# State products of late chunks in bank c, root products inside the second layer, a split first gate product

## The chip, the core and the metric

The kernel runs on one core of one Trainium2 chip. The metric is the device time of one execution in microseconds. A core has several engines with a queue of instructions each: TensorE (PE, matrix products; PEld are its weight loads), VectorE (DVE), ScalarE (ACT), GpSimd (POOL) and SyncE (SP, which here issues the loads and stores). Each engine takes its instructions in order and waits on semaphores for the others.

## What is computed

The program is an attention block with a decaying state, followed by a feed-forward block. All values are float32.

```python
# B, H, S, D = 4, 8, 768, 48
for t in range(S):
    kt, vt, rt = k[:, :, t], v[:, :, t], r[:, :, t]
    cur = einsum('bhd,bhe->bhde', u[None] * kt, vt)
    y[:, :, t] = einsum('bhd,bhde->bhe', rt, state + cur)
    state = w[None, :, :, None] * state + einsum('bhd,bhe->bhde', kt, vt)
x = y.transpose(0, 2, 1, 3).reshape(B * S, H * D)          # 3072 tokens of 384
xn = x / sqrt(mean(x * x, axis=-1) + 1e-6) * rms_g
g, val = xn @ w_gate, xn @ w_val                           # 384 -> 1536
out = (g * sigmoid(g) * val) @ w_out                       # 1536 -> 384
```

## The kernel before

**Chunks.** The 768 steps are cut into NS = 12 chunks of L = 64 steps; a chunk holds the four batches, so 256 tokens. For each chunk s, `mixing(s)` (line 814) does the attention. TensorE makes, under the names that the plan gives its operations: the scores A of decayed k against decayed r, the outputs Y (scores times V, plus r times the state ST), the mean of squares r for the norm, and the state products U (k, scaled per token as KH, against V), which update ST. Chunks 0 and 1 have in addition a product E for the bonus term u, and they get their roots through GpSimd, VectorE and a `spread` product; chunk 0 also makes a table of powers for the tokens with a product called wk. From chunk 2 on (`brief`) the squares are summed by VectorE, one product r with a matrix of ones follows, and ScalarE takes the roots. The normed chunk is kept in two halves of rows, `xa` and `xb`, where `xb` is `xa` with its halves of 64 partitions exchanged by ScalarE.

**Feed-forward.** For chunks 0 and 1, `gate_val` (line 1019) makes gate and value of 128 features at a time: six matmuls with `wa` and `xa` and six with `wb` and `xb` into one bank (`product`, line 665), each on half of the rows; the operations are called g. For the very first weights (chunk 0, quarter 0) the products use the outputs before the norm, `yT` and its exchanged copy `yb`, and the root is multiplied in afterwards. `project` (line 1049, operations P) applies w_out. From chunk 2 on, two chunks are done together by a seven-product scheme: `group(s, m)` (line 1120) has the products f1 to f7 for one block of features of chunks s and s + 1, and `second_layer(s)` (line 1157) the products P1 to P7.

**PSUM.** There are four tiles of two banks: `bank_a`, `bank_b`, `bank_c` for the products and `at` for the attention. E of chunk 1 uses a product bank; A, Y, U and r use `at`, which a key "at" guards as one.

**Order.** Each operation is put into a `Plan` (line 181) with an engine, a cost, what it reads and writes and a function that issues it. The list `ORDER` (line 83), written out by hand from a search, says in which order they are issued, so each engine's queue has that order. Where the plan sees TensorE idle in the start, `warm` (line 1104) puts products of a matrix of ones there. `hint` and `final` go with the last TensorE operations.

**Loads.** `loads(s)` (line 757) loads one chunk: `CH` (k and r by channel), `TOK` (by token) and `V`. At most four of these large loads are in flight. There is one buffer of each, so `V` of the next chunk can be loaded when the state products U of this one, its last readers, are done. The weights come in pieces as 64-bit numbers (`piece`, raw_0 to raw_5), which VectorE, ScalarE and GpSimd turn into float32; the first ones are loaded between the inputs of chunk 0. Later `check` reads weights again to look at their low bits.

**Where state products stand.** In `mixing(s)` U follows the norm of its chunk: it waits for KH and V and for the tile `at`, into which it writes, and VectorE adds it to ST from there. Y of the next chunk needs ST. The main loop (line 1276) does for each pair the token sums, the six groups, `mixing(s + 2)`, `loads(s + 3)`, `second_layer(s)`, `mixing(s + 3)`, `loads(s + 4)`; ORDER then interleaves these.

Of the kernel before, what the change touches and what calls it, by code (L numbers as in the profile page):

```python
# [49 lines left out]
P = 128  # L50
# [12 lines left out]
L = 64  # L63
# [9 lines left out]
def feature_order():  # L73
# [10 lines left out]
    0, 4, 7, 5, 6, 8, 1, 11, 41, 10, 2, 16, 3, 42, 43, 21, 45, 26, 12, 46, 44, 76, 47, 49, 31, 48, 51, 52, 17, 13, 53,  # L84
    14, 50, 54, 58, 15, 98, 59, 55, 9, 101, 56, 18, 60, 36, 22, 23, 28, 62, 65, 19, 61, 29, 66, 20, 57, 67, 83, 63,
    24, 64, 27, 68, 111, 84, 121, 116, 25, 69, 70, 32, 124, 71, 72, 33, 122, 77, 30, 85, 88, 78, 34, 73, 193, 106, 86,
    123, 79, 74, 102, 35, 127, 80, 125, 81, 100, 93, 82, 103, 37, 38, 126, 39, 75, 104, 89, 107, 40, 129, 203, 131,
    198, 128, 105, 132, 94, 130, 112, 108, 133, 109, 90, 208, 110, 189, 134, 153, 118, 135, 113, 154, 114, 119, 136,
    155, 137, 99, 117, 115, 192, 138, 194, 120, 148, 139, 161, 95, 156, 140, 157, 141, 158, 142, 195, 196, 159, 143,
    197, 144, 162, 160, 146, 165, 87, 205, 163, 145, 200, 169, 147, 199, 164, 190, 149, 166, 206, 201, 167, 150, 168,  # L90
    202, 287, 277, 151, 173, 191, 216, 174, 272, 213, 170, 175, 152, 210, 177, 171, 176, 204, 172, 209, 211, 304, 178,
    282, 91, 214, 309, 226, 181, 207, 215, 225, 179, 182, 92, 212, 185, 183, 222, 184, 180, 186, 239, 223, 217, 270,
    249, 283, 96, 274, 219, 245, 275, 220, 218, 273, 224, 269, 246, 187, 276, 314, 278, 221, 250, 188, 288, 284, 279,
    247, 227, 350, 248, 289, 228, 253, 351, 240, 290, 257, 231, 251, 229, 258, 232, 252, 280, 254, 285, 353, 324, 255,
    233, 319, 234, 261, 329, 256, 281, 230, 262, 235, 286, 242, 259, 263, 260, 271, 265, 241, 352, 362, 266, 97, 243,
    291, 359, 292, 264, 356, 244, 376, 293, 267, 360, 268, 410, 296, 354, 363, 310, 297, 306, 305, 307, 357, 311, 334,
    355, 312, 298, 409, 300, 308, 358, 339, 299, 361, 301, 313, 389, 302, 294, 303, 315, 236, 390, 316, 295, 393, 391,
    563, 320, 321, 394, 326, 327, 364, 322, 567, 365, 344, 392, 317, 325, 368, 366, 369, 318, 377, 367, 370, 564, 401,
    371, 331, 323, 372, 328, 335, 565, 379, 378, 332, 238, 402, 373, 340, 341, 330, 342, 395, 589, 569, 566, 596, 374,
    345, 411, 380, 333, 576, 572, 381, 336, 237, 337, 575, 338, 568, 573, 595, 346, 570, 343, 574, 375, 622, 571, 383,  # L100
    623, 347, 396, 384, 385, 624, 348, 577, 349, 625, 578, 397, 579, 581, 398, 582, 407, 441, 399, 420, 580, 408, 442,
    403, 632, 400, 412, 590, 413, 635, 591, 414, 583, 584, 626, 443, 415, 449, 444, 592, 631, 594, 404, 585, 629, 634,
    593, 386, 405, 627, 450, 406, 633, 446, 628, 451, 445, 447, 452, 448, 648, 455, 417, 453, 597, 654, 460, 456, 387,
    457, 462, 461, 454, 459, 468, 463, 458, 465, 469, 586, 464, 466, 470, 471, 479, 472, 467, 481, 480, 630, 418, 388,
    474, 475, 636, 476, 473, 478, 482, 638, 487, 477, 484, 488, 639, 649, 483, 485, 419, 637, 423, 490, 486, 655, 489,
    416, 493, 491, 498, 494, 500, 499, 640, 495, 641, 421, 497, 506, 492, 501, 799, 507, 642, 422, 503, 496, 643, 426,
    502, 504, 509, 505, 508, 424, 512, 510, 425, 517, 513, 511, 429, 803, 514, 519, 518, 588, 516, 525, 520, 800, 522,
    526, 515, 650, 521, 523, 427, 428, 528, 524, 432, 527, 531, 529, 530, 536, 532, 802, 533, 538, 537, 535, 534, 651,
    539, 544, 801, 652, 541, 545, 430, 431, 540, 542, 433, 547, 543, 434, 546, 806, 438, 550, 548, 435, 808, 555, 601,
    551, 653, 552, 549, 556, 553, 644, 602, 603, 804, 554, 645, 831, 605, 598, 646, 811, 812, 557, 439, 558, 587, 604,  # L110
    599, 809, 436, 810, 437, 562, 440, 825, 606, 609, 561, 647, 832, 656, 600, 805, 612, 610, 559, 560, 611, 807, 858,
    613, 608, 657, 614, 813, 615, 617, 616, 658, 618, 814, 619, 815, 817, 818, 862, 826, 660, 661, 819, 607, 859, 685,
    659, 687, 686, 620, 621, 693, 688, 690, 694, 820, 695, 689, 691, 664, 696, 692, 860, 699, 697, 698, 704, 700, 861,
    706, 705, 662, 701, 828, 870, 703, 707, 827, 708, 702, 663, 709, 867, 667, 712, 710, 665, 711, 715, 713, 868, 714,
    718, 716, 666, 717, 670, 723, 719, 721, 725, 724, 720, 722, 731, 726, 727, 732, 733, 668, 728, 669, 871, 673, 742,
    729, 730, 734, 884, 891, 737, 735, 743, 744, 738, 739, 671, 741, 750, 745, 829, 746, 751, 736, 752, 672, 747, 740,
    864, 676, 833, 761, 748, 749, 753, 756, 754, 762, 763, 757, 755, 1035, 758, 674, 769, 760, 764, 765, 770, 1036,
    675, 766, 771, 759, 780, 767, 768, 772, 830, 775, 773, 781, 776, 863, 774, 777, 869, 890, 782, 865, 779, 677, 788,
    783, 866, 785, 789, 778, 678, 784, 786, 682, 816, 679, 791, 787, 794, 792, 790, 793, 795, 872, 797, 796, 798, 834,
    837, 1037, 821, 1042, 838, 840, 839, 835, 683, 873, 836, 680, 681, 684, 822, 845, 876, 874, 877, 1038, 875, 1039,  # L120
    878, 841, 879, 846, 880, 1044, 881, 849, 842, 844, 1048, 882, 893, 883, 823, 894, 848, 1045, 850, 885, 886, 824,
    851, 887, 1047, 847, 852, 843, 853, 923, 1061, 854, 921, 895, 1068, 888, 922, 855, 896, 889, 924, 897, 856, 1040,
    1094, 1067, 926, 892, 857, 929, 927, 925, 930, 1041, 931, 932, 928, 940, 933, 1046, 935, 941, 1043, 942, 936, 937,
    898, 939, 948, 943, 944, 949, 934, 950, 899, 938, 945, 903, 900, 959, 946, 947, 951, 954, 952, 1098, 953, 1049,
    960, 955, 957, 956, 1051, 961, 958, 963, 962, 1050, 382, 1062, 964, 901, 967, 965, 966, 970, 968, 1053, 902, 1054,
    973, 904, 906, 969, 971, 905, 978, 974, 1097, 980, 979, 975, 972, 977, 982, 981, 1095, 1055, 1096, 1056, 983, 976,
    986, 984, 985, 1064, 987, 1063, 1120, 1069, 989, 909, 1103, 988, 992, 990, 1107, 1065, 991, 997, 993, 1106, 1066,
    994, 999, 998, 995, 1104, 996, 1099, 1000, 907, 1126, 1005, 1101, 1100, 1002, 1006, 1001, 1003, 908, 912, 1008,
    1004, 1127, 1007, 1011, 1009, 1010, 1016, 1012, 910, 1014, 1013, 1018, 1017, 1015, 911, 1020, 1019, 915, 1052,
    1275, 1021, 1024, 1022, 1023, 1027, 913, 1105, 914, 1102, 1030, 1025, 918, 1028, 1029, 1031, 1108, 1026, 1032,  # L130
    1033, 1034, 1073, 1070, 916, 917, 1071, 1121, 1074, 1122, 1057, 1076, 1109, 1058, 1112, 1059, 1271, 1075, 1081,
    1110, 1272, 1113, 919, 1111, 1072, 920, 1114, 1082, 1077, 1115, 1274, 1116, 1060, 1117, 1085, 1078, 1083, 1119,
    1079, 1273, 1080, 1281, 1118, 1084, 1086, 1278, 1129, 1277, 1130, 1280, 1087, 1123, 1089, 1124, 1157, 1090, 1088,
    1159, 1158, 1160, 1091, 1132, 1125, 1133, 1131, 1092, 1276, 1297, 1093, 1162, 1304, 1165, 1163, 1279, 1161, 1166,
    1136, 1128, 1303, 1168, 1164, 1167, 1171, 1169, 1170, 1176, 1172, 1282, 1173, 1178, 1177, 1175, 1283, 1180, 1284,
    1179, 1134, 1330, 1135, 1181, 1174, 1139, 1184, 1182, 1137, 1183, 1187, 1185, 1138, 1190, 1188, 1142, 1186, 1334,
    1197, 1191, 1195, 1331, 1192, 1196, 1285, 1194, 1189, 1198, 1332, 1287, 1203, 1193, 1200, 1140, 1288, 1204, 1339,
    1199, 1201, 1141, 1206, 1202, 1298, 1145, 1209, 1207, 1337, 1205, 1286, 1216, 1210, 1333, 1208, 1214, 1289, 1218,
    1215, 1290, 1212, 1211, 1143, 1222, 1213, 1144, 1217, 1148, 1223, 1291, 1224, 1219, 1233, 1220, 1146, 1221, 1225,
    1228, 1226, 1234, 1235, 1229, 1147, 1230, 1151, 1241, 1227, 1232, 1236, 1237, 1242, 1299, 1243, 1231, 1238, 1292,  # L140
# [40 lines left out]
class Plan:  # L181
# [48 lines left out]
    def give(self, order, free, idle, hint, final):  # L230

        assert sorted(order) == list(range(len(self.ops)))
        start, busy = self.times(order, free), 0.0
        last = [i for i in order if self.ops[i][0] == "PE"][-4:]
        for i in order:
            if i == last[0]:
                hint()
# [1565 lines left out]
```

## Time and profile before

| | |
|---|---|
| time, median of 3 runs | 597.23 us (596.34 to 598.35) |
| the profiled execution | 596.35 us |
| its span, first to last instruction | 594.6 us |
| granted TensorE clock | 0.997 |
| TensorE busy | 583.1 us, 7226 matmul records |
| VectorE, ScalarE, GpSimd busy | 419.0, 295.1, 42.6 us |
| moved by DMA | 62.99 MB |

The span is the time from the first to the last instruction of one profiled execution; its own time is a little longer. A float32 matmul leaves two records, so twelve records are six matmuls. A row of a timeline has the start, the length, the engine, the source line, the operation, "out<-in" by the names of the tiles, the form and the number of instructions; at its end, where the engine had been idle, the length of that and what ended it stand in brackets. The line is that of a helper (L178) throughout, so rows are told apart by their tiles. In a product's form, 64*128 means 64 rows and 128 columns of weights, and 64x256 the moved operand.

### The profile page before, as it was taken

What the parts mean: (1) busy time and instruction counts of PE and PEld (TensorE: products, weight loads), DVE (VectorE), ACT (ScalarE), POOL (GpSimd) and SP (SyncE); (2) the same over time, 40 slices, a digit from 0 to 9 for tenths busy, and PEclk for the clock granted to TensorE, in tenths of its full rate; (3) what the DMA queues carried; (4) which work ended last, traced back from release to release, by engine and by line L of the source; (5) the groups of instructions that cost most, each with busy time, mean ns of one, the idle gap of its engine ahead of it and who ended that gap; (6) DMA issues with size and microseconds to landing.
All of it is one profiled execution on the core that took longest, in us unless ns stands there. A gap on an engine that the chain in (4) does not pass through costs nothing.

```text
span 594.6 us, 16484 instructions
## 1 busy us (share of the span) xinstructions
PE 583.1 (98%) x7226; PEld 512.5 (86%) x7226; DVE 419.0 (70%) x622; ACT 295.1 (50%) x713; POOL 42.6 (7%) x40
## 2 busy tenths in 40 slices
PE   8899999999999999999999999999999999999995
PEld 6688887667888899888999888899888899988995
DVE  7869798988767887666885576796665676355641
ACT  6855784847266443743383267564364652131300
POOL 2443143210000000000000000000000000000000
PEclk9999999999999999999999999999999999999998
DMA  8866664231422143131404404302621201210001
GB/s 281 321 237 237 255 219 151 96 101 46 148 90 79 59 155 81 54 107 63 133 7 128 167 29 142 134 7 53 228 77 54 64 9 26 80 41 15 2 23 37
DMA packets 22768, 62.99 MB, mean 106 GB/s; under 512 B 2944, under 2 KB 9760, under 8 KB 21280
## 3 DMA queue, kind: packets, MB, share of 16 engines
q1 hardware_dynamic: 21920, 61.36, 30.9%
q8 instruction: 58, 0.95, 0.6%
q10 hardware_dynamic: 768, 0.49, 0.3%
q14 instruction: 22, 0.18, 0.1%
HBM read 56.04 MB, written 4.72 MB: 102 GB/s over the span
## 4 chain that ended last, share of the span: by engine, by line
PE 94%; DMA 2%; ACT 1%; DVE 1%; issue 0%; POOL 0%; SPq 0%; ACTq 0%; DVEq 0%; POOLq 0%
PE bank_b L178 32%; PE bank_a L178 27%; PE bank_c L178 25%; PE at L178 10%; DMA raw<-in_wkb_dram 1%; DMA raw<-in_wka_dram 1%; DMA chan<-in_chan_dram 0%; ACT ST L178 0%; DVE ms L178 0%; DVE KH L178 0%; POOL wb L178 0%; ACT ku L178 0%; ACT yT L178 0%; ACT wk L178 0%; POOL ms L178 0%
## 5 line engine op out<-in xcount | busy, mean ns | idle before, releaser
L178 DVE TENSOR_TENSOR gv<-bank_b,m 128x512 f32<-128x512 f32 x90 | 62.2, 691 | 60.5 <-PE bank_b L178 58.6
L178 ACT ACTIVATE gv<-gv 128x256 f32<-128x256 f32 (+1 forms) x60 | 31.0, 524 | 70.5 <-DVE gv L178 70.3
L178 DVE TENSOR_TENSOR gv<-bank_c,gv 128x512 f32<-128x512 f32 x60 | 41.5, 691 | 23.8 <-PE bank_c L178 23.2
L178 PE MATMUL bank_b<-xa,wa 64*128 64x256 f32 x444 | 55.1, 381 | 0.0
L178 ACT COPY m<-bank_a 128x512 f32<-128x512 f32 (+1 forms) x35 | 20.0, 571 | 64.2 <-PE bank_a L178 38.0
L178 PEld LDWEIGHTS bank_b<-xa,wa 64*128 64x128 f32 x444 | 42.1, 187 | 6.1 <-DVE TOK L178 0.7
L178 PE MATMUL bank_a<-xa,wa 64*128 64x256 f32 x372 | 46.2, 380 | 0.0
L178 PE MATMUL bank_a<-xb,wb 64*128 64x256 f32 x372 | 45.6, 378 | 0.0
L178 PE MATMUL bank_a<-wo,h 128*128 128x192 f32 x264 | 45.6, 329 | 0.0
L178 PE MATMUL bank_b<-t,s 64*128 64x256 f32 x360 | 44.3, 378 | 0.0
L178 PE MATMUL bank_b<-t,wb 64*128 64x256 f32 x360 | 44.0, 377 | 0.0
L178 PE MATMUL bank_c<-t,s 64*128 64x256 f32 x360 | 44.0, 377 | 0.0
L178 PE MATMUL bank_c<-xb,s 64*128 64x256 f32 x360 | 43.9, 376 | 0.0
L178 PEld LDWEIGHTS bank_a<-wo,h 128*128 128x128 f32 x264 | 42.9, 190 | 0.8 <-issue 0.3
L178 ACT ACTIVATE MT<-dmask,du 128x64 f32<-128x64 f32 x160 | 41.5, 340 | 3.5 <-DVE du L178 3.4
L178 ACT ACTIVATE rows_out<-rows_out 128x384 f32<-128x384 f32 x72 | 39.8, 559 | 0.5
L178 PEld LDWEIGHTS bank_a<-xb,wb 64*128 64x128 f32 x372 | 35.8, 187 | 4.5 <-issue 0.3
L178 PEld LDWEIGHTS bank_a<-xa,wa 64*128 64x128 f32 x372 | 35.3, 187 | 4.7 <-issue 0.6
L178 ACT ACTIVATE gv<-bank_a 128x256 f32<-128x256 f32 x30 | 11.5, 385 | 54.5 <-PE bank_a L178 54.5
L178 DVE TENSOR_TENSOR h<-gv 128x256 f32<-128x256 f32 (+1 forms) x60 | 32.5, 551 | 8.3 <-ACT gv L178 8.1
L178 PEld LDWEIGHTS bank_c<-xb,s 64*128 64x128 f32 x360 | 34.9, 187 | 4.0
L178 PEld LDWEIGHTS bank_b<-t,s 64*128 64x128 f32 x360 | 34.5, 187 | 4.3 <-issue 0.3
(183 smaller groups left out, 1099.6 us busy)
## 6 DMA issues: line engine op xcount, KB each, us to landing
chan<-in_chan_dram SPq DMA_DIRECT2D x11, 1024.0 KB, 5.7
TOK<-in_tok_dram SPq DMA_DIRECT2D x10, 768.0 KB, 4.3
V<-in_vpad_dram SPq DMA_DIRECT2D x12, 512.0 KB, 4.8
raw<-in_wot_dram SPq DMA_DIRECT2D x8, 576.0 KB, 5.6
rows_out<-in_wka_dram SPq DMA_DIRECT2D x12, 384.0 KB, 3.0
rows_out<-in_wkb_dram SPq DMA_DIRECT2D x12, 384.0 KB, 3.1
rows_out<-in_wot_dram SPq DMA_DIRECT2D x12, 384.0 KB, 3.4
raw<-in_wka_dram SPq DMA_DIRECT2D x6, 576.0 KB, 5.5
```

The lines of the kernel that those rows point to most:

```text
L178: return lambda *args, **kwargs: self.tc.keep_in_program_order(give(*args, **kwargs))
```

## The change

There are five edits and a new `ORDER`.

1. **State products apart from `mixing`.** `mixing` is cut into `mixing` (attention, squares and, for odd late chunks, the root product), `roots_of` (the sums of squares, the root product and the roots), `mixed` (norm and exchange) and `state` (decay of the state, U, the additions). For chunks 3 and later, `state` takes the tile `bank_c` and its keys in place of `at`. It is added after group 0 of a pair for the odd chunk and after group 2 (`SLOT`) for the even chunk, whose `mixing` also moves there.
2. **Root product of even chunks.** For even chunks from 4 on, `roots_of` is called within `second_layer`, just before P5, and writes half of bank b.
3. **Loads.** `V` of a chunk from 4 on is loaded after the state products before it (`load_values`), no longer within `loads`.
4. **First gate product.** With `SPLIT = 1` the first product of chunk 0 is given as four operations: the `wa` side for batches 0 and 1, then for 2 and 3, then the `wb` side likewise, each of six matmuls with 128 columns. `yb` gets keys of its own per pair of batches.
5. **Fillers and hint.** The fillers before the first data are 128 columns wide and four times as many; `unused` has another letter order; the branch hint comes one TensorE operation later.

```diff
-        last = [i for i in order if self.ops[i][0] == "PE"][-4:]
+        last = [i for i in order if self.ops[i][0] == "PE"][-3:]
...
-    def product(ps_, w, x, start):
+    def product(ps_, w, x, start, cols=slice(0, NT)):
...
-                    ps_[:, z, 0:NT], w[rows, cc, :], x[rows, cc, :], start=start and cc == 0,
+                    ps_[:, z, cols], w[rows, cc, :], x[rows, cc, cols], start=start and cc == 0,
...
-        add("SP", 1.5, [], ["V"], lambda: load_v(s), land=LAND, name=f"load v {s}")
         if s == max(EARLY) + 1:
             add("SP", 0.5, [], ["utab"], load_u, land=LAND)
+        if s < 4:
+            load_values(s)
+
+    def load_values(s):
+        add("SP", 1.5, [], ["V"], lambda: load_v(s), land=LAND, name=f"load v {s}")
...
-        bank, key = next_at()
+        bank, key = next_at() if s < 4 or s % 2 else (None, None)
...
+            if s < 4 or s % 2:
+                roots_of(s, bank, key)
...
+        if not brief:
+            mixed(s)
+            state(s)
+        elif s < NS - 1:
+            add("DVE", 0.95, ["TOKk", "wk"], ["KH"], lambda: state_k(s), port=True, name=f"h {s}")
+
+    def roots_of(s, bank, key):
+        for n in (2, 1):
+            add(
+                "DVE", 0.15 + 0.27 * n, ["sq1"], ["sq0"],
+                lambda n=n: dve.tensor_add(sq[:, 0:n], sq[:, 0:n], sq[:, n : 2 * n]), port=True, name=f"q {s}",
+            )
+        add(
+            "PE", 0.45, ["sq0", "sq1"], [key],
+            lambda: pe.matmul(bank[:, 0:NT], ones, sq[:, 0], start=True, stop=True), name=f"r {s}",
+            rows="full",
+        )
+        def roots():
+            act.activation(rms, bank[:, 0:NT], AF.Sqrt, scale=1.0 / DM, bias=eps)
+            silu_table()
+
+        add("ACT", 3.3, [key], ["diag"], roots, land=-TABLE, name=f"sqrt {s}")
+        add("DVE", 1.75, [], ["diag"], lambda: dve.reciprocal(rms, rms), name=f"inv {s}")
+
+    def mixed(s):
+        x = place(s)
+        if s > 1:
+            add("DVE", 0.95, ["diag", "yT0", "yT1"], [f"xa{x}"], lambda: scaled(s, rms, yT), port=True, name=f"x {s}")
         for z in range(2):
             add("ACT", 0.83, [f"xa{x}"], [f"xb{x}.{z}"], lambda z=z: exchange(s, z), name=f"xb {s}")
+
+    def state(s, tile=at, keys=("at", "at")):
...
-        next_at(), next_at()
-        add("PE", 0.97, ["KH", "V"], both, lambda: states(at), name=f"U {s}", rows="4")
+        if keys[0] == "at":
+            next_at(), next_at()
+        add("PE", 0.97, ["KH", "V"], list(keys), lambda: states(tile), name=f"U {s}", rows="4")
...
+    SPLIT = 1
...
+        if first and o < SPLIT:
+            for q in range(2):
+                cols, own = slice(2 * L * q, 2 * L * (q + 1)), [f"{keys[0]} {q}"]
+                add(
+                    "PE", 0.66, weight_keys("wa", i, o) + [f"yT{q}"] + [f"{keys[0]} 0"] * q, own + keys * (1 - q),
+                    lambda q=q, cols=cols: product(ps_, wa[i][:, o], yT, q == 0, cols), name=f"g {s} {i} {o}", rows=True,
+                )
+            for q in range(2):
+                cols, own = slice(2 * L * q, 2 * L * (q + 1)), [f"{keys[0]} {q}"]
+                add(
+                    "PE", 0.66, weight_keys("wb", i, o) + [f"yb{q}"], own,
+                    lambda cols=cols: product(ps_, wb[i][:, o], yb, False, cols), name=f"g {s} {i} {o}", rows=True,
+                )
+            keys = keys + [f"{keys[0]} {q}" for q in range(2)]
...
-    unused = list("bbaaacbbbbbb")
+    unused = list("baaaacbbbbbb")
...
-            for _ in range(int((until + 0.4 - 3.75) / 0.86)):
-                pe.matmul(bank[:, 0], ones, free_dims(ones, (0, 4), (1, P)), start=True, stop=True)
+            for _ in range(4 * int((until + 0.4 - 3.75) / 0.86)):
+                pe.matmul(bank[:, 0, 0:P], ones, ones, start=True, stop=True)
...
         if not last:
+            roots_of(s + 2, bank_of["b"][:, 1], "b")
+            mixed(s + 2)
             mm("z", gs + out_keys("o1"), sum_1, w2(0), True, "P5")
...
+    SLOT = 2
...
             group(s, m)
+            if m == 0:
+                state(s + 1, bank_of["c"], bank_keys["c"])
+                if s + 2 < NS:
+                    load_values(s + 2)
+            if m == SLOT and s + 2 < NS:
+                mixing(s + 2), state(s + 2, bank_of["c"], bank_keys["c"]), load_values(s + 3)
...
-            mixing(s + 2), loads(s + 3)
+            loads(s + 3)
...
-            mixing(s + 3)
+            mixing(s + 3), mixed(s + 3)
```

In the order that results, U of chunks 3, 6, 7 and 9 stands directly before the scores A of the chunk after it, U of chunk 8 directly behind the outputs Y of its own chunk, and U of chunk 10 behind A of chunk 11. In the start the products U0, E1 and A1 follow each other (before: E1, U0, a gate product, A1), the second half of the first gate product stands behind `spread` and wk, and SP's queue has two weight pieces ahead of V of chunk 0 (before: one).

## The prediction

> **What bounds the kernel now.** I read the busy times by stage first, then TensorE's timeline in the middle, then the timelines of the start. In the stage view the columns are the stretch, its length, and the busy time (and instruction count) of TensorE, its weight loads, VectorE, ScalarE and GpSimd, then clock, DMA share and GB/s.
>
> ```profile
> 0.00:36.00 36.00, 31.31 (x676) 24.02 (x677) 29.75 (x68) 24.33 (x57) 13.63 (x22) 1.00 0.86 302
> 36.00:588.00 552.00, 551.78 (x6554) 488.44 (x6550) 388.87 (x554) 270.82 (x657) 28.99 (x19) 1.00 0.29 94
> 588.00:594.60 6.60, 0.04 (x1) 0.00 (x0) 0.36 (x1) 0.00 (x0) 0.00 (x0) 0.78 0.14 38
> ```
>
> From 36 us to 588 us TensorE is idle for 0.22 us. There is no wait to remove in 552 us: there the time is what TensorE's instructions take, and only their cost or their order can change it. The first 36 us have 4.7 us of idle TensorE, with the DMA engines at 0.86. The last 6.6 us are stores and the end of the program, which the diff leaves alone.
>
> Order has a price. TensorE works in three forms: products on two halves of 64 rows (shown as 64*128), attention work on blocks of 64 or 48 rows and columns (48*64, 64*64, 48*48), and whole-array work (128*128). The timeline (start, length, instruction) around chunk 5's root product:
>
> ```profile
> 173.45 1.46 PE L178 MATMUL bank_b<-t,s 64*128 64x256 f32 x12
> 174.75 1.46 PE L178 MATMUL bank_a<-third,wb 64*128 64x256 f32 x12
> 176.14 0.70 PE L178 MATMUL at<-sq,ones 128*128 128x256 f32 x2
> 176.77 1.57 PE L178 MATMUL bank_b<-xa,wa 64*128 64x256 f32 x12
> 178.17 1.46 PE L178 MATMUL bank_c<-t,s 64*128 64x256 f32 x12
> ```
>
> Lengths overlap, so steps from start to start count. A product between products takes 174.75 - 173.45 = 1.30. The one before the root product takes 1.39, the root product 0.63, the one after it 1.40. The same view in the second layer, where a root product stands among whole-array work, and where state products (at<-V,KH) stand alone:
>
> ```profile
> 303.92 0.59 PE L178 MATMUL at<-sq,ones 128*128 128x256 f32 x2
> 304.35 4.06 PE L178 MATMUL bank_a<-wo,h 128*128 128x192 f32 x24
> 308.25 4.06 PE L178 MATMUL bank_b<-wo,h 128*128 128x192 f32 x24
> 312.15 4.06 PE L178 MATMUL bank_a<-w,h 128*128 128x192 f32 x24
> 316.14 1.15 PE L178 MATMUL at<-V,KH 64*64 64x48 f32 x64
> 317.22 1.57 PE L178 MATMUL bank_b<-t,s 64*128 64x256 f32 x12
> 318.62 1.46 PE L178 MATMUL bank_a<-xa,wa 64*128 64x256 f32 x12
> ```
>
> There the root product takes 0.43. So a stay of it between products costs 0.63 - 0.43 + 0.09 + 0.10 = 0.40 for two changes of form, 0.20 each. The state products alone take 1.08 and lengthen their neighbours by 0.09 (3.99 for 3.90) and 0.10. Of their 1.08 about 0.14 is entering and leaving (the 64 records start 0.93 us apart, first to last, and the next instruction 0.15 later, where a group of the same form follows within 0.04). A stay in the attention form costs 0.34, or 0.17 per change.
>
> **The change, part by part. 1, order in the saturated stretch.** I count the changes of form in the order in which each program gives TensorE its work, from the first product of the second weight quarter on (35.0 us in the profile). Before: 82. After: 69. Between products and attention work they go from 39 to 38, between products and whole-array work from 22 to 21, between whole-array and attention work from 21 to 10. Six stays in the attention form vanish, because state products U are given beside scores A or outputs Y (U3 A4, U6 A7, U7 A8, Y8 U8, U9 A10, A11 U10), and even chunks' root products move beside second-layer work. Sum: 1 x 0.20 + 12 x 0.17 = 2.2 us less. The work itself is the same instructions, nothing covers this time, so all of it comes off the span if no wait takes its place.
>
> A rule of the Trainium skill bears on such merging. "Runtime: NRT & Kernel Launch", section "Instruction fetch mechanics", says that an engine's program comes in blocks of 16 KiB, 256 instructions, that the sequencer fetches ahead by DMA, and that this is mostly hidden. The page of this kernel shows the queue, 58 packets with 0.95 MB, 16 KB each, some 128 matmul records and their weight loads to a block:
>
> ```profile
> q8 instruction: 58, 0.95, 0.6%
> ```
>
> In the start it is not hidden. Two groups are cut in the middle, with nothing named as releaser:
>
> ```profile
> 13.31 0.67 PE L178 MATMUL bank_c<-MT,V 64*64 64x64 f32 x27 [0.57 <-issue]
> ...
> 29.13 0.81 PE L178 MATMUL at<-RR,chan 48*64 48x64 f32 x39 [0.71 <-issue]
> ```
>
> The two cuts are 254 matmul records apart, two blocks, so I take them for late blocks. Two blocks took 15.8 us; the second begins 127 records after 13.31, which counts to the middle of chunk 1's scores E, about 23.9, and took 5.3 us. A merged U and A is 128 records in 2.0 us, so a whole block can pass in little more than that. By the rule this costs nothing; by the row of the start it would cost up to 3 us each. In the saturated stretch the DMA share is 0.29 instead of 0.86, and outputs Y (128 records in 1.99 us) stand there ten times without a cut. I take 0 there, and keep the row for the start.
>
> **2, the start.** Here the change costs. (a) V of chunk 0 is loaded after two weight pieces instead of one, and first outputs wait for it already (0.44 us until 9.78, put down to that load). The queue:
>
> ```profile
> 3.90 0.33 SPq L178 DMA_DIRECT2D raw<-in_wka_dram  x1
> 4.85 0.33 SPq L178 DMA_DIRECT2D V<-in_vpad_dram  x1
> 5.55 0.33 SPq L178 DMA_DIRECT2D raw<-in_wkb_dram  x1
> ```
>
> A piece of 384 KB at the stage's 302 GB/s is 1.3 us, and issues there follow each other after 0.7 to 1.75, so V lands about 1 us later. Its outputs, then the scores and outputs of the second pair behind them in TensorE's queue, slip by as much. Of this the cut of 0.57 at 13.31 can absorb a part: +0.3 (0 to +1.0).
> (b) The first gate product is given by pairs of batches, and its second half (the xb side) now stands behind the spread and the table product wk. Before, this half ran at 17.01 to 18.50, while the mean square went through VectorE and GpSimd (spread at 20.05 after a wait of 0.83 for diag). Nothing else fills that hole, so 1.5 us move behind wk (21.21): +1.5. There they cover the wait of U0 for KH, 0.61 until 25.07: -0.6. By column count the halves cost the same (12 matmuls of 128 columns for 6 of 256). No row has 64*128 with 128 columns; the whole-array 128x128 filler takes 0.22 per matmul, half of the root product's 0.43, so I take +0.1, with +1.3 per side if the 12 weight loads hold it.
> (c) U0, E1 and A1 now follow each other: 192 records in 3 us, one and a half blocks, where one took 5.3 us. Before, a product of 1.66 stood between them and 0.71 + 0.17 was still lost at A1. I take 0.3 more than before (between -0.9, if the blocks fall well, and +2).
> Together +0.3 + 1.5 - 0.6 + 0.1 + 0.3 = +1.6. The twelve 128-column fillers at the very start replace three of 512 columns, the same columns, ahead of the first data: 0.
>
> **3, what is late next.** V and TOK of late chunks are now loaded after that chunk's state product, so their load starts when U ends. The tightest place is chunk 10: between the end of U9 and Y10 stand A10 and five products, 1.1 + 5 x 1.3 + 0.2 = 7.8 us. The page gives for the load:
>
> ```profile
> V<-in_vpad_dram SPq DMA_DIRECT2D x12, 512.0 KB, 4.8
> ```
>
> Behind the load on SP stand TOK, a weight check and chan; what they feed is needed later. With half a microsecond to issue, 5.3 of 7.8: hidden, 0, and about +1 if that load takes twice its median. The next tightest (U5 to Y6) has seven products between, 9.3 us. U in bank c needs c drained by VectorE first: at least one product stands between c's last writer and U, 1.3 us against one read of 0.69 (gv<-bank_c,gv). U's own three additions into ST (0.55 each, 1.7 together) then have at least two products, 2.7 us, before bank c is written again (tightest at U4). Both are hidden as long as VectorE, busy for 389 of 552 us, is not a microsecond behind; where it is, each place would cost a few tenths, and there are eight. The end differs only in where the branch hint is placed.
>
> **Sum.** -2.2 + 1.6 = -0.6. The profiled execution was 596.35 with a span of 594.6, so 1.75 lies outside it; after, span 594.0 and execution 595.8. The three runs have a median of 597.23 (596.34 to 598.35), 0.9 above the profiled one, and I forecast on their scale: 597.2 - 0.6 = 596.6.
>
> **Rivals.** *The start hides its losses* (0.26): blocks fall well, A1's 0.71 and 0.17 vanish and V's delay goes into the cut, so the start costs at most 0.3. For it: both cuts and U0's wait, 1.9 us together, are idle time that another order can fill. Against it: the hole of 17 to 20 us stays. Time: 597.2 - 2.2 + 0.2 = 595.2.
> *Instruction blocks in the start* (0.24), the one on the other side: U0, E1, A1 use up a block within 2.5 us of its beginning and TensorE waits till 5.3 us have passed, 2.8 lost where 0.9 was lost before, and the halves of the first product, which double their instructions, bring the next boundary forward into Y1 with another 1 to 2. Start +4.0, time 597.2 - 2.2 + 4.0 = 599.0; it decides once the start costs more than 2.2 + 1.8 = 4.0, and is slower at all from 2.2.
> *V10 late* adds 1 us to any case; alone it ends at 597.6 and is counted with no change.
> *No net effect*: the switches do not cost where I think, because TensorE would wait for VectorE or ScalarE instead. Against it: they are busy for 389 and 271 of 552 us. It lies within the likeliest case.
>
> **How the numbers follow.** A measurement of this kernel tells about 0.3% (1.8 us) from no change. The likeliest case, a start of +0.5 to +3.5, ends within it: 595.5 to 598.5, chance 0.50. Of the first rival some ends just inside, of the third case some just outside; I give faster 0.26, same 0.50, slower 0.24. Range: from 594.8 (start costs nothing, fewer switches at 0.20 each) to 598.8 (start +3.8).
>
> **What would show it.** Right: between 45 us and the last matmul no idle on TensorE, and that stretch about 2.2 us shorter for the same work; the first product of chunk 1 begins 1 to 2 us later than its 45.8 (after one U of 1.1 more in front of it); second halves of the first gate product behind wk; waits put down to issue in E1 or A1. Wrong: a wait of TensorE for V, KH or bank c in the saturated stretch, a start that ends no later than before, or cuts of the issue kind at merged U and A.

## The result and the profile after

The changed kernel takes 594.81 us (median of 20 runs, 593.09 to 597.04). The kernel before takes 597.75 us (20 runs, 595.33 to 600.69; the three shown ahead of the prediction are among them). The ratio is 0.9952, with a 95% interval of 0.9937 to 0.9966: 0.48% or 2.9 us faster, and the whole interval lies beyond the 0.3% that a measurement can tell from no change. I had forecast -0.6 us.

The profiled execution after took 594.46 us with a span of 592.7 us, against 596.35 and 594.6 before: 1.9 us less in each. The traces explain these 1.9 us. The other 1.0 us of the medians' difference is in neither: the profiled execution before was 1.40 us below the median of its 20 runs, the one after 0.35 us below.

The middle stage of the kernel after, in the columns of the prediction's stage view:

```profile
36.00:586.00 550.00, 549.39 (x6554) 491.29 (x6551) 384.99 (x554) 270.02 (x657) 28.94 (x19) 1.00 0.29 95
```

TensorE still sets the time: it is idle for 0.61 us of the middle 550 (0.22 of 552 before). Fixed times do not cut the two programs at the same work, so I cut both where the same TensorE operations are left: before at the first product of chunk 1 (45.80), after at U1, which stands in front of it now (46.33), and at the start of the last matmul group (583.98 and 582.75). Before:

```profile
0.00:45.80 45.80, 41.11 (x756) 32.22 (x758) 34.67 (x82) 29.31 (x70) 18.63 (x25) 1.00 0.78 272
45.80:583.98 538.18, 537.96 (x6449) 476.48 (x6446) 382.35 (x536) 265.84 (x644) 23.99 (x15) 1.00 0.28 93
583.98:594.60 10.62, 4.06 (x25) 3.77 (x24) 1.96 (x6) 0.00 (x0) 0.00 (x0) 0.86 0.18 48
```

After:

```profile
0.00:46.33 46.33, 42.12 (x811) 37.06 (x811) 37.04 (x82) 31.95 (x78) 18.81 (x25) 1.00 0.82 292
46.33:582.75 536.42, 535.81 (x6448) 479.67 (x6447) 376.79 (x537) 261.86 (x636) 23.09 (x15) 1.00 0.28 91
582.75:592.70 9.95, 4.07 (x26) 3.77 (x24) 1.43 (x4) 0.00 (x0) 0.00 (x0) 0.86 0.17 46
```

The second column gives the three differences: start +0.53, saturated stretch -1.76, end -0.67, together -1.90.

| part | forecast | in the traces |
|---|---|---|
| start | +1.6 | +0.53 |
| saturated stretch | -2.2 | -1.76 |
| end | 0 | -0.67 |
| sum | -0.6 | -1.90 |

**The saturated stretch.** TensorE's timeline of the kernel after, around U3, where scores now follow directly:

```profile
145.15 1.46 PE L179 MATMUL bank_b<-t,s 64*128 64x256 f32 x12
146.54 1.15 PE L179 MATMUL bank_c<-V,KH 64*64 64x48 f32 x64
147.51 1.13 PE L179 MATMUL at<-RR,chan 48*64 48x64 f32 x64
148.56 1.57 PE L179 MATMUL bank_a<-third,wb 64*128 64x256 f32 x12
```

The same view around U4, which stands alone in both kernels:

```profile
167.69 1.46 PE L179 MATMUL bank_b<-t,s 64*128 64x256 f32 x12
169.08 1.15 PE L179 MATMUL bank_c<-V,KH 64*64 64x48 f32 x64
170.16 1.57 PE L179 MATMUL bank_a<-third,wb 64*128 64x256 f32 x12
```

From start to start, U alone takes 170.16 - 169.08 = 1.08, and A alone 1.09 at every place of both traces where it has no neighbour of its form. Side by side they take 148.56 - 146.54 = 2.02. The product in front of a stay takes 1.39 and the one behind it 1.40, where a product among products takes 1.30. A stay less between two products is thus worth 1.08 + 1.09 - 2.02 + 0.09 + 0.10 = 0.34, the forecast's figure. Y8 with U8 takes 2.91 (alone 3.07) and A11 with U10 2.01 (alone 2.17), so these two come to 0.35 each by the same reckoning. At this price six stays are 4 x 0.34 + 2 x 0.35 = 2.1 us, forecast 12 x 0.17 = 2.04.

Root products of even chunks, now at the edge of the second layer; the root product of chunk 9 stands within it, as r7, r9 and r11 did before:

```profile
383.61 0.70 PE L179 MATMUL bank_b<-sq,ones 128*128 128x256 f32 x2
384.15 4.06 PE L179 MATMUL bank_a<-wo,h 128*128 128x192 f32 x24
...
395.85 0.59 PE L179 MATMUL at<-sq,ones 128*128 128x256 f32 x2
396.28 4.06 PE L179 MATMUL bank_a<-wo,h 128*128 128x192 f32 x24
```

The first takes 0.54, the second 0.43. Between products it had taken 0.63 with 0.19 more in its neighbours.

**One late block.** The saturated stretch lost something back behind the pair Y8 and U8. TensorE's timeline there:

```profile
350.82 1.10 PE L179 MATMUL bank_c<-V,KH 64*64 64x48 f32 x64
351.85 1.57 PE L179 MATMUL bank_a<-xa,wa 64*128 64x256 f32 x12
353.25 0.38 PE L179 MATMUL bank_b<-t,s 64*128 64x256 f32 x1
354.24 1.35 PE L179 MATMUL bank_b<-t,s 64*128 64x256 f32 x10 [0.61 <-issue]
355.42 0.38 PE L179 MATMUL bank_a<-xb,wb 64*128 64x256 f32 x1
```

This product (f2 of group 3) takes 355.42 - 353.25 = 2.17 where a product between products takes 1.30: 0.87 lost in the middle of its matmuls, with no releaser. Counting all of TensorE's instructions in the trace (matmuls, weight loads and those of its sequencer) in blocks of 256, at the phase that the two cuts of the prediction give, a block begins at 350.06, within Y8, and the next at 354.24, where work resumes. By this count all six cuts of the issue kind in the two traces (13.31, 29.13 and 33.98 before; 27.08, 32.52 and 354.24 after) stand at the edge of a block, to one instruction, and at each of them TensorE resumes 1.26 to 1.64 us after the end of an instruction packet. So the cuts are waits for instructions. SP's queue ahead of the late one:

```profile
348.02 0.80 SPq L179 DMA_DIRECT2D rows_out<-in_wka_dram  x2
```

The queues in the DMA view of 350.06 to 351.80 (packets, megabytes, share of the 16 engines):

```profile
q1 hardware_dynamic: 215, 0.56, 82.2%
```

The same view of 351.8 to 352.8:

```profile
q8 instruction: 1, 0.02, 5.8%
```

Two loads of 384 KB for the weight check are issued at 348.02 and 348.39. In the 1.74 us from 350.06 the data queue has 0.82 of the engines and no instruction packet starts. One is served from 351.80 to 352.74, and TensorE resumes 1.50 later. Without the loss this block would take 3.3 us. Two blocks as short passed without a cut: the one from 447.00, which holds the end of A11 and U10 (3.20 us), and the one from 80.22 (3.37 us). Their packets start 0.19 and 0.24 us after the block, this one 1.74. So a short block alone does not cost; this one was short and its packet late. Data alone does not make a packet late either, since the data queue had 0.98 of the engines from 80.0 to 80.5. Whether the two loads delayed this packet was not tried.

Three other items of this stretch are not a price of order. The late block is +0.87. In group 5, f5 takes 1.57 in front of the scores A9, where 1.39 is usual: +0.18; the first weight load of A9 stands idle for 0.33 us, which the profile puts down to ScalarE (rows_out, the weight check). And a wait of the root product r3 is gone: P of chunk 0 in front of it took 4.36 before and takes 3.96 after, -0.40. In the plan r3 waits for ScalarE's reading of `at`, done at 102.95, and for VectorE's two sums of squares, done at 104.30; the profile names a ScalarE step on ST that ends just then, which r3 does not need. TensorE, GpSimd and VectorE before:

```profile
104.44 0.67 PE L178 MATMUL at<-sq,ones 128*128 128x256 f32 x2 [0.22 <-ACT ST L178]
100.78 4.77 POOL L178 TENSOR_TENSOR wo<-bits,ulp 128x576 int32<-128x576 int32 x3 [9.20 <-DVE bits L178]
101.27 3.02 DVE L178 TENSOR_TENSOR sq<-sq 128x512 f32<-128x512 f32 x2 [0.63 <-ACT sq L178]
```

The two sums of squares take 1.48 and 1.51 us beside weight sums of GpSimd. In the kernel after, chunk 3's take 0.69 and 0.42 (at 118.46 and 119.94), with GpSimd idle.

What is left of -1.76 is -1.76 + 0.40 - 0.87 - 0.18 = -2.41, the effect of order; the forecast had -2.24 for it. By steps from start to start, 0.89 of it lies in A, Y and U themselves, 0.53 in the root products, and the rest in the products and P next to them. It belongs to the 13 changes of form fewer, and cannot be booked pair by pair: U7 and A8, say, each stood between whole-array work and a product before, where a change of form remains when they leave.

**The start.** The cuts in the middle of a group after the change:

```profile
27.08 0.46 PE L179 MATMUL bank_a<-chan,ku 48*64 48x64 f32 x16 [0.65 <-issue]
...
32.52 0.81 PE L179 MATMUL at<-MT,V 64*64 64x64 f32 x41 [0.74 <-issue]
```

There are two. Before there were three (0.57 in the second outputs, 0.71 in A1, 0.17 in Y1); now they stand in E1 and Y1. Both were named as places in the forecast. They are 127 matmul records apart (16 of E1, 64 of A1, 24 of two products, 23 of Y1), one block; by the count of instructions blocks begin at 22.94, 27.09 and 32.52, so 4.15 and 5.43 us apart, near the 5.3 us of the prediction.

V of chunk 0 in SP's queue, and the first outputs on TensorE:

```profile
4.00 1.45 SPq L179 DMA_DIRECT2D raw<-in_wka_dram  x2
6.30 0.33 SPq L179 DMA_DIRECT2D V<-in_vpad_dram  x1
...
11.54 0.91 PE L179 MATMUL at<-MT,V 64*64 64x64 f32 x48 [0.80 <-DMA V<-in_vpad_dram]
```

V is issued 1.45 us later (6.30 for 4.85) and its outputs start 1.76 later (11.54 for 9.78). The mean-square products, 13.91 before, start at 14.85: +0.94 are left, since the cut of 0.57 in the second outputs is gone.

Then comes the part that I had not looked at, the way from the mean square to the spread. GpSimd and VectorE of the kernel before:

```profile
14.98 1.18 POOL L178 TENSOR_TENSOR wb<-bits,ulp 128x384 int32<-128x384 int32 x1 [3.82 <-DVE bits L178]
15.52 0.16 DVE L178 TENSOR_SCALAR ms<-at 128x2 f32<-128x2 f32 x1 [0.21 <-PE at L178]
15.59 0.99 DVE L178 SCALAR_TENSOR_TENSOR bits<-raw,bits 128x384 int32<-128x384 int32 x1
16.12 1.02 POOL L178 TENSOR_TENSOR ms<-ms,minus_half 128x2 f32<-128x2 f32 x1
17.11 1.00 POOL L178 TENSOR_TENSOR wa<-bits,ulp 128x384 int32<-128x384 int32 x1
17.18 0.95 DVE L178 TENSOR_TENSOR ms<-ms 128x2 f32<-128x2 f32 x1 [0.60 <-POOL ms L178]
18.07 1.00 POOL L178 TENSOR_TENSOR wb<-bits,ulp 128x384 int32<-128x384 int32 x1
18.16 0.92 DVE L178 TENSOR_TENSOR ms<-ms 128x2 f32<-128x2 f32 x1
```

And after:

```profile
16.46 0.16 DVE L179 TENSOR_SCALAR ms<-at 128x2 f32<-128x2 f32 x1 [0.28 <-PE at L179]
16.70 0.70 POOL L179 TENSOR_TENSOR ms<-ms,minus_half 128x2 f32<-128x2 f32 x1 [0.94 <-DVE ms L179]
17.37 1.00 POOL L179 TENSOR_TENSOR wa<-bits,ulp 128x384 int32<-128x384 int32 x1
17.44 0.94 DVE L179 TENSOR_TENSOR ms<-ms 128x2 f32<-128x2 f32 x1 [0.82 <-POOL ms L179]
18.42 0.16 DVE L179 TENSOR_TENSOR ms<-ms 128x2 f32<-128x2 f32 x1
```

The work is the same: mean square, a power on GpSimd, a refinement of two numbers per row on VectorE. Before, the power waits behind the sum of a weight piece (0.60 from ms to power; after, 0.24). It takes 1.02 beside a weight step of VectorE, and 0.70 alone. Both refinement steps before run beside a weight sum of GpSimd and take 0.95 and 0.92; after, only the first has one beside it (0.94), and the second takes 0.16. So 0.36 + 0.32 + 0.76 = 1.44 us less, and mean square to spread takes 19.55 - 16.46 = 3.09 in place of 4.53. The spread starts 0.50 earlier than before, although everything in front of it is 0.94 later.

A rule of the Trainium skill fits these rows. "SBUF — State Buffer", section "SBUF: two separate sides", says that VectorE and GpSimd share one pair of ports as an exclusive lock: a VectorE instruction with two SBUF inputs and a GpSimd instruction that reads SBUF block each other for the whole length of the one that came first. The three slow refinement steps end within 0.1 us of the end of the sum beside them (18.13 and 18.11, 19.08 and 19.07, 18.38 and 18.37), and the operation that costs 0.16 alone costs 0.92 to 0.95 there. A VectorE step that reads PSUM (ms<-at, 15.52) takes 0.16 although a sum runs beside it. The same refinement of chunk 1 is a check the other way round, since there the new order puts a sum beside the first step and the old one has none. Before, then after:

```profile
41.09 0.36 DVE L178 TENSOR_TENSOR ms<-ms 128x2 f32<-128x2 f32 x2
...
39.90 1.40 POOL L179 TENSOR_TENSOR wb<-bits,ulp 128x576 int32<-128x576 int32 x1
39.97 1.35 DVE L179 TENSOR_TENSOR ms<-ms 128x2 f32<-128x2 f32 x1 [0.81 <-POOL ms L179]
```

The step takes 0.16 without a sum and 1.35 with one, to within 0.02 us of the sum's end (41.32 and 41.30). A start where no sum is issued in the stretch of chunk 0 was not run.

**The end.** VectorE's last addition and SP's last issue of a store, before:

```profile
587.03 2.76 SPq L178 DMA_DIRECT2D out_dram<-rows_out  x2
588.08 0.36 DVE L178 TENSOR_TENSOR rows_out<-bank_a,rows_out 128x192 f32<-128x192 f32 x1 [1.33 <-PE bank_a L178]
```

After:

```profile
585.81 1.98 SPq L179 DMA_DIRECT2D out_dram<-rows_out  x2
586.86 0.36 DVE L179 TENSOR_TENSOR rows_out<-bank_a,rows_out 128x192 f32<-128x192 f32 x1 [0.95 <-PE bank_a L179]
587.25 0.51 ACTq L179 DMA_DIRECT2D out_dram<-rows_out  x1
```

In both, the last store can be issued when the last addition ends (588.44 and 587.22). After, the two last issues start at 587.24 and 587.25, at once. Before, one SP issue begun at 587.03 takes 2.12, and the last store is issued at 589.25, 0.81 late. Why it took so long is not shown; the kernel after has issues as long (2.15 on ScalarE's queue at 578.93, 1.34 on SP at 585.81), but none delays a store there. The span ends 5.35 us after the last issue before, 5.45 after. The new order gives the P7 product ahead of P3 at the end (before: P3, P7, P5; after: P7, P3, P5), so stores start at 581.79 in place of 584.96, and the nine issues that stood in the last 4.3 us before are eight spread over 5.5.

### The profile page after: what moved, and what is told of

Its sections match the earlier page's. It is cut to its first block, busy times and chain, and to the rows that moved or that the text cites. A ratio compares the mean times of both kernels' runs of the same rounds, so it can differ in the third digit from the quotient of the medians.

```text
span 592.7 us, 16598 instructions
## 1 busy us (share of the span) xinstructions
PE 582.0 (98%) x7280; PEld 520.5 (88%) x7280; DVE 415.3 (70%) x622; ACT 293.8 (50%) x713; POOL 41.9 (7%) x40
## 4 chain that ended last, share of the span: by engine, by line
PE 95%; DMA 2%; DVE 1%; issue 1%; ACT 0%; SPq 0%; POOL 0%; DVEq 0%
PE bank_b L179 33%; PE bank_c L179 27%; PE bank_a L179 27%; PE at L179 8%; DMA V<-in_vpad_dram 1%; DMA chan<-in_chan_dram 1%; DVE ms L179 0%; DVE KH L179 0%; ACT ku L179 0%; SPq L179 0%; ACT wk L179 0%; POOL ms L179 0%; ACT diag L179 0%; DVE rows_out L179 0%; DVE diag L179 0%
## 5 line engine op out<-in xcount | busy, mean ns | idle before, releaser
L179 ACT ACTIVATE gv<-gv 128x512 f32<-128x512 f32 (+1 forms) x60 | 30.8, 522 | 74.9 <-DVE gv L179 74.7
L179 PEld LDWEIGHTS bank_c<-t,s 64*128 64x128 f32 x360 | 35.8, 187 | 3.5
```

What stands on the lines that cost most here:

```text
L179: return lambda *args, **kwargs: self.tc.keep_in_program_order(give(*args, **kwargs))
```

## Experiments

No kernel was run beside the two. What stands above is read from one trace of each, with two helps. Where one trace holds the same operation in two settings (U beside A and alone, a refinement step beside a sum and alone), it is its own comparison, repeated at several places for the forms and at four for the refinement. And the prediction named places and sizes before the trace was seen. The causes that rest on a single place are argued, not shown. Three edits would have told them apart; none was tried.

The first, in the kernel before, takes the weight step out of VectorE's way between mean square and inverse, and with it one weight sum on GpSimd, by these places of its operations in the order:

```diff
-bits1 3, bits2 1, bits2 3, ms 0, bits2 2, inv 0, diag 0
+bits1 3, bits2 1, bits2 2, ms 0, inv 0, diag 0, bits2 3
```

If the sums make the refinement long, its two steps take 0.95 and 0.16, and the spread comes some 0.8 to 1.1 us earlier; whether that reaches the end depends on U0's wait for KH.

The second, in the kernel after, sets the six U one product away from A or Y, at the price that the rows give: 6 x 0.34 = +2.0 us, less what the late block at Y8 then gives back.

The third, in the kernel after, moves ScalarE's two check steps of that place behind U8, and with them the two loads of 384 KB:

```diff
-look 17, look 18, U 8, S 8, S 8
+U 8, S 8, S 8, look 17, look 18
```

If the packet waits for these loads, f2 takes 1.30 and the program 0.9 us less; if something else makes the packet late, the loss stays.

## Why the prediction was right or wrong

The direction was right and the size was not: -0.6 was forecast, -2.9 measured, and no measurable change had the highest chance. The time lies inside the range (594.8 to 598.8) by 0.01 us, and that is luck: the range stood on the 597.23 of three runs, and as a difference its lower end is -2.4, which the 20 runs of each pass with -2.9. The case that came nearest is the first rival, "the start hides its losses" (595.2). Of its reasons only one came, V's delay going into the cut; the loss at A1 moved to E1 and Y1 and did not vanish.

- **What bounds the kernel**: right. TensorE is busy throughout in both, and the order of its work made most of the change in the middle.
- **Order in the saturated stretch (-2.2)**: right in mechanism and near in size. A stay less between products is worth 0.34 in the trace after, as in the one before, and the 13 changes of form fewer make -2.4 us, against -2.2 forecast.
- **Instruction blocks there (0)**: wrong once. Ten Y in the trace before that passed without a cut said nothing on a Y directly followed by U when the block's packet comes late. The rule of the Trainium skill ("Runtime: NRT & Kernel Launch", "Instruction fetch mechanics") that crossing a block is mostly hidden holds for the other blocks of this stretch, where no wait of TensorE is put down to issue, and the one where it does not hold cost 0.87 us. The five pairs of U and A, the place that I had named as a sign of being wrong, went without a cut. A gain that I had left out, the 0.40 of r3's wait, made up for nearly half.
- **V of chunk 0 (+0.3, 0 to +1.0)**: right in mechanism, at the upper end: +0.94 at the mean-square products. I had V about 1 us later; it was 1.45 in the queue and 1.76 at the outputs. The cut did absorb its 0.57.
- **The second half of the first gate product (+1.5)**: right, 1.60 behind wk (0.77 and 0.83). Its split cost nothing that can be seen: a half takes 0.77 where half of a whole one with the same surroundings takes 0.75.
- **Its cover of U0's wait (-0.6)**: it covered 0.24; a wait of 0.37 for KH stays. KH starts when ScalarE has wk (23.08) and then takes 1.44 beside a weight sum of GpSimd (22.52 to 23.70), where it takes 0.95 alone; by my estimate from these figures it would else have ended at 24.03, before TensorE was free for U0 at 24.20.
- **U0, E1, A1 together (+0.3)**: by steps the cuts behind wk are 0.97 in A1 and 0.38 in Y1 before, 0.70 in E1 and 0.97 in Y1 after: +0.32. Right, and in the places named. The rival of instruction blocks had both places, but its sizes, 2.8 and 1 to 2, did not come. I missed that the three together are also one stay in the attention form less, -0.34, since I counted changes of form from 35.0 us on only.
- **Missed in the start: GpSimd's and VectorE's queues (-1.44)**. This is the step that failed. The forecast says of the hole from 17 to 20 us that it stays, and takes the length of the mean square's way as given. The new order also moves weight steps and sums on VectorE and GpSimd out of it. Both queues were in the order; I had followed SP's and TensorE's. The 0.40 of r3's wait in the middle is the same thing missed a second time. With +0.94, -1.44, +1.60, -0.24, +0.32 and -0.34, the start comes to +0.84; the last -0.31 are in the products of the start around E1 and U0 (1.50 and 1.66 before, 1.30 and 1.39 after). Of this 0.17 is a wait of A1 for the tile `at`, which ScalarE's copy of U0 held until 27.75 before; now E1 stands between the two.
- **Fillers (0)**: right in effect, not as argued. The same columns took longer: twelve fillers of 128 columns 5.33 us, three of 512 columns 4.51, and the first E starts at 6.41 in place of 5.59. That was hidden, because the first outputs wait for V.
- **Late V, TOK and bank c (0)**: right. The waits of TensorE after the change hold no row for bank c, and V only in the start. The page gives 5.3 us to landing for V, against the 4.8 that I used and the 7.8 at the tightest place:

```profile
V<-in_vpad_dram SPq DMA_DIRECT2D x12, 512.0 KB, 5.3
```

- **The end (0)**: wrong, -0.67. I wrote that the diff leaves it alone and that the end differs only in the branch hint. The order of the last products changed, and with it when the stores are issued; that this made the one issue shorter is argued, not shown.
- **Open**: 1.0 us of the 2.9 lies between the executions, not between the two traces. One trace of each cannot say whether the start before varies more (its 20 runs spread over 5.4 us, those after over 4.0).

## What to carry to other kernels

A price read from neighbouring rows of the trace before (0.34 us for a stay in another form) held to a hundredth wherever the neighbours were the same; count the changes and multiply (-2.2 forecast, -2.4 measured). A reordering by hand changes every queue, so go through each engine's list for every stretch that waits on a chain across engines. The largest missed term here was a power and two refinements of two numbers per row, stretched from 3.1 to 4.5 us by weight work next to them, and the same kind of neighbour made r3 wait. Look at the last products and their stores too, since an issue that starts just before the last result is ready delays the last store by what is left of it.

## What was not expected of the hardware

A VectorE step on 128x2 elements takes 0.16 us alone and 0.92 to 0.95 us beside a GpSimd sum of 128x384, 1.35 us beside one of 128x576, to the sum's end. The issue of a store took 0.47 us on SP at its shortest in the last 20 us and 2.12 us once, just ahead of the last store of the kernel before. TensorE stood for 0.57 to 0.74 us at five block edges, and once for 0.17, until 1.26 to 1.64 us after the end of an instruction packet; one of them, in a stretch with a DMA share of 0.28, cost 0.87 us.
